# Slot sums copied and turned in halves, products in quarters with row products between, and one copy for the last outputs

## The chip, the cores and the metric

The kernel runs on one core of a Trainium2 chip. The metric is the device time of one execution in microseconds (us); of several runs the median is given. Five engines with an instruction queue each run beside one another: PE (matrix products; PEld is its weight load), DVE (vector), ACT (scalar functions and copies), POOL (a second elementwise engine) and SP, which here issues most loads and stores. Each engine takes its instructions strictly in the order in which the program gives them, and waits where one of them needs a result of another engine or of a transfer.

## The reference

Three layers stand one behind the other, all in float32:

```python
# 1 attention over 4 x 8 heads, 1152 keys, queries pooled by 2 (576), head size 64
attn_out = softmax(scale * mean_of_2(q) @ k.T) @ v          # -> x: 2304 tokens x 512
# 2 soft mixture of experts: 8 experts of 4 slots (32 slots), inner size 1024
logits = x @ phi
slot_input = softmax_over_tokens(logits).T @ x              # 32 x 512
slot_out[e] = relu(slot_input[e] @ w1[e]) @ w2[e]           # 32 x 512
x = softmax_over_slots(logits) @ slot_out                   # 2304 x 512
# 3 a gated layer, inner size 2048
h = x @ w_in
out = (h * cos(h)) @ w_out                                  # 2304 x 512
```

## The kernel before

The kernel doesn't form `x` of layer 3. Since `x @ w_in = softmax_over_slots(logits) @ (slot_out @ w_in)`, it computes the 32 x 2048 products `slot_out @ w_in` once (divided by 2 pi, tiles `Pst0` to `Pst3` of 512 columns each, with a rounded part and the rest stacked along the partitions) and multiplies them by the token weights `cT`.

Layers 1 and 2 are recorded by `attention()`; the order of their operations is written out in the string `ORDER`. At the end of layer 2 stand three operations that the change touches: `so_copy` copies the slot sums (32 slots, spread over four groups of partitions, 512 columns) from PSUM to SBUF (`so`), `so_turn` turns them by four products with a selection matrix (`gsel`), and `so_put` copies the result to SBUF as `soT`, four blocks of 128 x 128, one for each 128 of the 512 rows of `w_in` (index `kk`).

Layer 3 follows the table `START` for its beginning, and then a loop. The letters of the table:

- `p` (`p_some`): products of `soT` with the first 256 columns of `w_in` (`win_q`), in two column blocks of 128, in full width of the partitions. Each block is copied to `Pst0` by ACT, and its rest is formed by DVE.
- `r` (`p_rows`): the products of a whole half of `w_in`'s columns as four row groups of 32 partitions, ending in `p_hi` (ACT) and `p_lo` (DVE).
- `q` (`p_put`): spreads these by two products for each 256 columns (`s_hi`, `s_lo`) and copies them to a `Pst`.
- `s` (`split_w`): splits one of 16 blocks of `w_out` into a rounded part `w_hi` and the rest `w_lo`, on engines that `SPLIT` names: for blocks 0, 1, 2 `w_hi` is ACT's, `w_lo` is DVE's for 0 and POOL's for 1 and 2, and for block 3 `w_hi` is DVE's and `w_lo` POOL's.
- `u` (`emit_u`): product of `cT` and `Pst` for a unit of 128 or 256 inner columns and 256 tokens; ACT makes `t` from it, DVE `r`.
- `g` (`emit_g`): sine and square of `r` on ACT, `g` and its rounded part `hi` on DVE, the rest `lo` on POOL.
- `o` (`emit_o`): three products for each 128 inner columns and 128 tokens (`hi` with `w_hi`, `hi` with `w_lo`, `lo` with `w_hi`), summed over all units of a block of 256 tokens; at its end `store` copies the sums and sends them out.

All loads of layer 3 are issued by SP in the order of the program. The lines with their numbers:

Of the kernel before, what the change touches and what calls it, by code (L numbers as in the profile page):

```python
# [8 lines left out]
FP32 = mybir.dt.float32  # L9
# [22 lines left out]


START = (
# [106 lines left out]
def kernel(  # L141
# [77 lines left out]
    def mx():  # L219
        return mx2()[:, 0]  # L220

    def mx2():
        return ps_2.tile([128, 2, 512], FP32, tag=f"s{cur[0].spot}", name="mx")
# [804 lines left out]

    def so_copy(i):
        sh["so"] = ep.tile([128, DM], FP32, tag=f"E{cur[0].spot}", name="so")  # L1030
        nc.scalar.activation(out=sh["so"], in_=sh["o"], func=AF.Copy)

    def so_turn(i):
        sh["s"] = mx()
        for kk in range(HP):
            nc.tensor.matmul(
                out=sh["s"][:, kk * 128:(kk + 1) * 128], lhsT=sh["so"][:, kk * 128:(kk + 1) * 128],
                rhs=gsel.rearrange("p g s -> p (g s)"), start=True, stop=True,
            )

    def so_put(i):
        sh["soT"] = ep.tile([128, HP, 128], FP32, tag=f"E{cur[0].spot}", name="soT")
        nc.vector.tensor_copy(out=sh["soT"].rearrange("p k s -> p (k s)"), in_=sh["s"])

    def c_zero(b):
        sh["c", b] = mx()
# [449 lines left out]
    with tc.manual_schedule():  # L1496
# [51 lines left out]
        def load_win_q(f):  # L1548
            t = wo.tile([128, HP, 512], FP32, tag=f"w_lo{2 + f}", name="win_q")
            nc.sync.dma_start(out=t, in_=w32q[f])  # L1550
            for kk in range(HP):
                win_q[f, kk] = t[:, kk]
# [18 lines left out]

        for f in range(2):
            load_win_q(f)
            load_w(f, 2 - f)
        for i in range(HP // 2):
            nc.sync.dma_start(out=win1[:, i], in_=w32p[i].rearrange("p a b c -> p a (b c)"))

        ph = {}

        def p_some(f, c0, c1, pm):  # L1580
            pm = pm[:, 0:c1 - c0]
            for kk in range(HP):
                nc.tensor.matmul(
                    out=pm, lhsT=soT[:, kk, :],
                    rhs=win_q[f, kk][:, c0:c1], start=(kk == 0), stop=(kk == HP - 1),
                )
            nc.scalar.activation(out=Pst[f][:, c0:c1], in_=pm, func=AF.Copy, scale=INV2PI)
            lo = Pst[f][64:128, c0:c1]
            nc.vector.scalar_tensor_tensor(
                out=lo, in0=pm[64:128], scalar=INV2PI, in1=lo.bitcast(FP32), op0=ALU.mult, op1=ALU.subtract  # L1590
            )

        def p_rows(r, pm):
            pm = pm[:, 0:256]
            for kk in range(HP):
                for g in range(4):
                    c0 = g % 2 * 256
                    x = win1[:, kk // 2, kk % 2, g // 2 * 512 + c0:g // 2 * 512 + c0 + 256] if r else win_q[g // 2, kk][:, c0:c0 + 256]
                    nc.tensor.matmul(
                        out=pm[32 * g:32 * g + 32], lhsT=soT[:, kk, 0:32], rhs=x, start=(kk == 0), stop=(kk == HP - 1),  # L1600
                    )
            hi, lo = [op.tile([128, 256], F32R, bufs=1, tag=n, name=n) for n in ("p_hi", "p_lo")]
            nc.scalar.activation(out=hi, in_=pm, func=AF.Copy, scale=INV2PI)
            nc.vector.scalar_tensor_tensor(
                out=lo, in0=pm, scalar=INV2PI, in1=hi.bitcast(FP32), op0=ALU.mult, op1=ALU.subtract
            )
            ph[r] = hi, lo
# [58 lines left out]
        def emit_o(i):  # L1666
            blk, f0, n = units[i]
            hi, lo = gs.pop(i)
            last = i == len(units) - 1

            def product(s, f, part):
                ff = f0 + f
                if ff == 0 and part == 0:
                    acc[blk, s] = ps_o.tile([128, DM], FP32, tag=f"o{s}", name=f"o{s}")
                o = acc[blk, s]
                x = (lo if part else hi)[:, f, s * 128:(s + 1) * 128]
                nc.tensor.matmul(out=o, lhsT=x, rhs=w_hi[ff], start=(ff == 0 and not part), stop=bool(part and ff == NF - 1))  # L1677
                if not part:
                    nc.tensor.matmul(out=o, lhsT=x, rhs=w_lo[ff], start=False, stop=False)  # L1679

            def store(s):
                o = acc.pop((blk, s))
                ob = op.tile([128, DM], FP32, tag="ob", name="ob")
                if last:
                    h = DM // 2
                    nc.scalar.activation(out=ob[:, 0:h], in_=o[:, 0:h], func=AF.Copy, scale=-TWOPI)
                    nc.vector.tensor_scalar(out=ob[:, h:], in0=o[:, h:], scalar1=-TWOPI, scalar2=None, op0=ALU.mult)
                else:
                    nc.scalar.activation(out=ob, in_=o, func=AF.Copy, scale=-TWOPI)

                if blk < 2 * B:
                    runs = [(blk // 2, blk % 2 * TB + s * 128, 128)]
                else:
                    runs = [(2 * s + c, 512, 64) for c in range(2)]
                r0 = 0
                for b, c0, n in runs:
                    while n:
                        j, p0 = divmod(c0, QP)
                        w = min(n, QP - p0)
                        (nc.scalar if last and s and r0 else nc.sync).dma_start(  # L1700
                            out=out[b * SQ:(b + 1) * SQ, :].rearrange("(p j) d -> j p d", j=QJ)[j][p0:p0 + w],
                            in_=ob[r0:r0 + w],
                        )
                        r0, c0, n = r0 + w, c0 + w, n - w

            todo = [(s, f, part) for part in range(2) for f in range(n) for s in range(2)]
            for x in sorted(todo, key=lambda x: x[0]) if last else todo:
                product(*x)
                if last and x[1:] == (n - 1, 1):
                    store(x[0])  # L1710
            if f0 + n == NF and not last:
                for s in range(2):
                    store(s)

        def bank(i):
            return ps_o.tile([128, DM], FP32, tag=f"o{i}", name="pm")

        def emit_p(*a):
            p_some(*a, bank(1))

        def emit_r(r):
            p_rows(r, bank(0))
            if r == 0:
                for i in range(2, 4):
                    load_w(i)

# [49 lines left out]
```

## Time and profile before

| what | value |
|---|---|
| median of 3 runs | 733.82 us (733.76 to 736.04) |
| the profiled execution's own time | 736.87 us |
| its span, first to last instruction | 735.1 us |
| PE busy | 719.3 us (98%) |
| DVE, ACT, POOL busy | 573.0, 449.3, 418.5 us |

A profile is one execution with every instruction's start and duration. The span is a little shorter than the time of the same execution, and both may differ from the median of the runs, so a difference that is worked out from the profile is added to the median. A PE that is busy for 98% of the span is no proof that PE is at its peak everywhere: its instructions overlap, and what counts for an edit are the few places where PE waits.

### The profile page before, as it was taken

Reading aid. Unit: us, or ns where it says so; the run is one execution under the profiler, and the core shown is the slowest. Engines: PE = TensorE matmul, PEld = TensorE weight load, DVE = VectorE, ACT = ScalarE, POOL = GpSimd, SP = SyncE. Lnnn points to the kernel's source line nnn. Section 1 sums busy time; section 2 is a strip of 40 time slices with the busy share of each in tenths; the row PEclk is TensorE's granted clock in tenths of the full one; section 3 lists DMA queues with packets and bytes.
Section 4 is the critical chain, followed back from the end, with each engine's and each line's share of the span. In section 5 each row is a group of like instructions: output and inputs, shape, how many; then the busy total and the mean of one; then the engine's idle time right before and its main releaser. Section 6 shows DMA issues by size and latency. Waiting matters only on the chain.

```text
span 735.1 us, 16465 instructions
## 1 busy us (share of the span) xinstructions
PE 719.3 (98%) x6428; PEld 531.0 (72%) x6428; DVE 573.0 (78%) x917; ACT 449.3 (61%) x846; POOL 418.5 (57%) x351
## 2 busy tenths in 40 slices
PE   8999999999999999999999999998999999999997
PEld 7677767767677776777777676434778888888886
DVE  6999999989999999999999977404876665656562
ACT  5566666576566676567576555325676566666661
POOL 5676686775877746695767551314854444444442
PEclk9999999999999999999999999999999999999999
DMA  8455665575548646554633555999010010100101
GB/s 203 102 153 137 167 174 144 156 186 155 157 131 247 163 127 175 165 158 134 182 107 83 197 192 196 400 409 418 37 29 29 0 30 29 29 4 26 30 29 29
DMA packets 75970, 101.48 MB, mean 138 GB/s; under 512 B 47156, under 2 KB 47540, under 8 KB 74996
## 3 DMA queue, kind: packets, MB, share of 16 engines
q1 hardware_dynamic: 69872, 100.09, 44.9%
q10 hardware_dynamic: 6020, 0.34, 0.6%
q8 instruction: 51, 0.84, 0.5%
q14 instruction: 27, 0.22, 0.1%
HBM read 87.10 MB, written 13.11 MB: 136 GB/s over the span
## 4 chain that ended last, share of the span: by engine, by line
PE 82%; DVE 7%; DMA 4%; ACT 3%; issue 2%; POOL 2%; SPq 0%; ACTq 0%; POOLq 0%; DVEq 0%
PE mx L576 18%; PE o L1677 16%; PE mx L533 14%; PE o L1679 8%; PE mx L487 6%; PE mx L536 4%; PE u L1641 2%; DVE nm L496 2%; PE mx L990 2%; PE mx L514 2%; PE mx L447 1%; PE mx L606 1%; DMA w<-in_moe_w_dram 1%; PE mx L422 1%; PE mx L1023 1%
## 5 line engine op out<-in xcount | busy, mean ns | idle before, releaser
L565 POOL TENSOR_TENSOR ES<-ES,E 128x576 f32<-128x576 f32 (+2 forms) x154 | 224.5, 1459 | 66.3 <-DVE ES L565 39.3
L496 DVE TENSOR_REDUCE nm<-mx 128x2 f32<-128x768 f32 x240 | 221.4, 950 | 18.2 <-PE mx L487 16.9
L547 ACT ACTIVATE E<-mx 128x576 f32<-128x576 f32 (+2 forms) x288 | 174.8, 652 | 66.1 <-PE mx L536 46.1
L533 PE MATMUL mx<-Q,kX 64*128 64x288 f32 (+2 forms) x1152 | 164.3, 302 | 1.1 <-DVE nm L496 0.7
L576 PE MATMUL mx<-E,vn 128*64 128x288 f32 (+2 forms) x1152 | 158.0, 413 | 0.7 <-ACT part L818 0.4
L1661 POOL TENSOR_TENSOR lo<-g,hi 128x512 fp32r<-128x512 f32 (+1 forms) x73 | 94.0, 1287 | 109.3 <-DVE hi L1659 103.1
L533 PEld LDWEIGHTS mx<-Q,kX 64*128 64x128 f32 x1152 | 110.2, 184 | 13.7 <-issue 3.5
L576 PEld LDWEIGHTS mx<-E,vn 128*64 128x64 f32 x1152 | 75.3, 136 | 57.9 <-ACT E L547 5.8
L1677 PE MATMUL o<-w_hi,hi 128*128 128x512 f32 x288 | 113.0, 392 | 0.6 <-DVE hi L1659 0.6
L1679 PE MATMUL o<-w_lo,hi 128*128 128x512 f32 x288 | 113.1, 393 | 0.3 <-DVE w_lo L1568 0.3
L533 PE MATMUL mx<-Q,kY 64*128 64x288 f32 (+2 forms) x576 | 88.0, 292 | 0.0
L536 PE MATMUL mx<-NM,one_row 64*128 64x288 f32 (+2 forms) x576 | 87.8, 291 | 0.0
L487 PE MATMUL mx<-kX,Q 64*128 64x384 f32 x490 | 83.0, 368 | 0.9 <-ACT kX L460 0.6
L1646 ACT ACTIVATE t<-u 128x512 f32<-128x512 f32 (+1 forms) x73 | 42.9, 591 | 58.5 <-PE u L1641 58.4
L1657 DVE SCALAR_TENSOR_TENSOR g<-r,u 128x512 f32<-128x512 f32 (+1 forms) x73 | 49.6, 679 | 36.0 <-ACT r L1655 34.7
L1677 PE MATMUL o<-w_hi,lo 128*128 128x512 f32 x288 | 77.3, 389 | 0.0
L1648 DVE SCALAR_TENSOR_TENSOR r<-t,u 128x512 f32<-128x512 f32 (+1 forms) x73 | 49.3, 678 | 35.4 <-ACT t L1646 34.9
L319 POOL TENSOR_TENSOR cvt<-cvt 128x512 uint32<-128x512 uint32 x32 | 43.2, 1349 | 54.1 <-ACT E L547 19.4
L1677 PEld LDWEIGHTS o<-w_hi,lo 128*128 128x128 f32 x288 | 54.1, 188 | 11.3
L1677 PEld LDWEIGHTS o<-w_hi,hi 128*128 128x128 f32 x288 | 54.1, 188 | 10.8 <-DVE hi L1659 0.8
L1679 PEld LDWEIGHTS o<-w_lo,hi 128*128 128x128 f32 x288 | 54.2, 188 | 10.2 <-DVE w_lo L1568 0.6
L487 PEld LDWEIGHTS mx<-kX,Q 64*128 64x128 f32 x490 | 43.3, 184 | 23.0 <-issue 9.2
(231 smaller groups left out, 1023.5 us busy)
## 6 DMA issues: line engine op xcount, KB each, us to landing
w<-in_moe_w_dram SPq DMA_DIRECT2D x42, 512.0 KB
vn<-in_v_dram SPq DMA_DIRECT2D x16, 576.0 KB
qn<-in_q_dram SPq DMA_DIRECT2D x15, 576.0 KB
kn<-in_k_dram SPq DMA_DIRECT2D x15, 576.0 KB
raw<-in_moe_w_in_dram SPq DMA_DIRECT2D x16, 512.0 KB
raw<-in_moe_w_out_dram SPq DMA_DIRECT2D x16, 512.0 KB
hw<-in_moe_w_dram SPq DMA_DIRECT2D x23, 256.0 KB
lw<-in_moe_w_dram SPq DMA_DIRECT2D x10, 512.0 KB
```

The lines of the kernel that those rows point to most:

```text
L487: nc.tensor.matmul(out=m[:, h, 0:384], lhsT=Q1[p % 2][hs, AT[i]:AT[i] + 128], rhs=X[p][hs, ks], start=True, stop=True)
L496: nc.vector.tensor_reduce(out=nm3[p][:, i, :, c:c + 1], in_=m[:, :, 0:384], axis=AX.X, op=ALU.max)
L533: nc.tensor.matmul(out=sc[:, h, 0:n_q], lhsT=x[hs, ks], rhs=y[hs, qs], start=(n == 0), stop=False)
L536: nc.tensor.matmul(out=sc[:, h, 0:n_q], lhsT=one_row[hs, :], rhs=NM[p % 2][hs, qs], start=False, stop=True)
L547: nc.scalar.activation(out=e, in_=sc[:, :, 0:n_q], func=AF.Exp, scale=1.0 / 16.0)
L565: eng.tensor_tensor(out=ES[p, a], in0=ES[p, a], in1=E[p, a, t], op=ALU.add)
L576: nc.tensor.matmul(out=av_t[p, a, g][64 * h:64 * h + 64, 0:n_q], lhsT=vn[p][:, h, t, :], rhs=E[p, a, t][:, h, :], start=(t == g), stop=(t ...
L1648: nc.vector.scalar_tensor_tensor(out=r, in0=t, scalar=MAGIC, in1=u, op0=ALU.subtract, op1=ALU.subtract)
L1657: nc.vector.scalar_tensor_tensor(out=g, in0=r, scalar=1.0, in1=u, op0=ALU.subtract, op1=ALU.mult)
L1661: nc.gpsimd.tensor_tensor(out=lo[:, 0:n], in0=g, in1=hi[:, 0:n].bitcast(FP32), op=ALU.subtract)
L1677: nc.tensor.matmul(out=o, lhsT=x, rhs=w_hi[ff], start=(ff == 0 and not part), stop=bool(part and ff == NF - 1))
L1679: nc.tensor.matmul(out=o, lhsT=x, rhs=w_lo[ff], start=False, stop=False)
```

## The change

`so_copy` makes two copies of 256 columns on ACT. `so_turn` writes the four turned blocks to two banks of PSUM. `so_put` makes two copies of 256 columns, the first on ACT, the second on DVE. The first 256 columns' products (`p_first`) run over the first two `kk` for both column blocks and then over the last two. The row products of `r` 0 are split over `START`: one `kk` ahead of the first `u`, one ahead of the second, and two behind it; the entries `s` 1, `s` 2 and `s` 0 come later than the two `u`. Both halves of `win_q` are loaded first, the `w_out` blocks behind them. `store` copies the last outputs in one piece on ACT, as all others.

```diff
 START = (
-    ("s", 1), ("p", 0, 0, 128), ("s", 2), ("p", 0, 128, 256), ("u", 0), ("s", 0), ("u", 1), ("g", 0),
-    ("r", 0), ("s", 3), ("g", 1), ("q", 0, 1), ("q", 1, 2), ("u", 2), ("o", 0), ("s", 5), ("s", 6), ("s", 4), ("u", 3),
+    ("p",), ("r", 0, 0, 1), ("u", 0), ("s", 1), ("r", 0, 1, 2), ("u", 1), ("s", 2), ("s", 0), ("g", 0),
+    ("r", 0, 2, 4), ("s", 3), ("g", 1), ("q", 0, 1), ("q", 1, 2), ("u", 2), ("o", 0), ("s", 5), ("s", 6), ("s", 4), ("u", 3),
...
     def so_copy(i):
         sh["so"] = ep.tile([128, DM], FP32, tag=f"E{cur[0].spot}", name="so")
-        nc.scalar.activation(out=sh["so"], in_=sh["o"], func=AF.Copy)
+        for j in range(2):
+            cs = slice(j * DM // 2, (j + 1) * DM // 2)
+            nc.scalar.activation(out=sh["so"][:, cs], in_=sh["o"][:, cs], func=AF.Copy)
 
     def so_turn(i):
-        sh["s"] = mx()
+        sh["s"] = mx2()
...
-                out=sh["s"][:, kk * 128:(kk + 1) * 128], lhsT=sh["so"][:, kk * 128:(kk + 1) * 128],
+                out=sh["s"][:, kk // 2, kk % 2 * 128:(kk % 2 + 1) * 128], lhsT=sh["so"][:, kk * 128:(kk + 1) * 128],
...
-        nc.vector.tensor_copy(out=sh["soT"].rearrange("p k s -> p (k s)"), in_=sh["s"])
+        for j in range(2):
+            o, x = sh["soT"][:, 2 * j:2 * j + 2].rearrange("p k s -> p (k s)"), sh["s"][:, j, 0:256]
+            if j:
+                nc.vector.tensor_copy(out=o, in_=x)
+            else:
+                nc.scalar.activation(out=o, in_=x, func=AF.Copy)
...
         for f in range(2):
             load_win_q(f)
+        for f in range(2):
             load_w(f, 2 - f)
...
+        def p_first(pms):
+            for k0 in (0, 2):
+                for c, pm in enumerate(pms):
+                    cs = slice(128 * c, 128 * c + 128)
+                    for kk in range(k0, k0 + 2):
+                        nc.tensor.matmul(
+                            out=pm[:, 0:128], lhsT=soT[:, kk, :], rhs=win_q[0, kk][:, cs], start=(kk == 0), stop=(kk == HP - 1),
+                        )
+            for c, pm in enumerate(pms):
+                cs = slice(128 * c, 128 * c + 128)
+                nc.scalar.activation(out=Pst[0][:, cs], in_=pm[:, 0:128], func=AF.Copy, scale=INV2PI)
...
-        def p_rows(r, pm):
+        def p_rows(r, pm, k0=0, k1=HP):
             pm = pm[:, 0:256]
-            for kk in range(HP):
+            for kk in range(k0, k1):
...
+            if k1 < HP:
+                return
...
-                if last:
-                    h = DM // 2
-                    nc.scalar.activation(out=ob[:, 0:h], in_=o[:, 0:h], func=AF.Copy, scale=-TWOPI)
-                    nc.vector.tensor_scalar(out=ob[:, h:], in0=o[:, h:], scalar1=-TWOPI, scalar2=None, op0=ALU.mult)
-                else:
-                    nc.scalar.activation(out=ob, in_=o, func=AF.Copy, scale=-TWOPI)
+                nc.scalar.activation(out=ob, in_=o, func=AF.Copy, scale=-TWOPI)
```

The order of ACT's instructions from the slot sums' copy to `p_hi`, before (`w_hi1` is block 1's rounded part; `pm`, `mx` and `u` lie in PSUM):

```order
L1031 ACTIVATE so_7807<-mx_7710 128x512
L1566 ACTIVATE w_hi1_7851<-w_lo_7868 128x512
L1587 ACTIVATE Pst0_7835<-pm_7885 128x128
L1566 ACTIVATE w_hi2_7852<-w_lo_7868 128x512
L1587 ACTIVATE Pst0_7835<-pm_7894 128x128
L1646 ACTIVATE t_7903<-u_7901 128x256
L1566 ACTIVATE w_hi0_7850<-w_lo_7868 128x512
L1646 ACTIVATE t_7911<-u_7909 128x256
L1654 ACTIVATE r_7905<-r_7905 128x256
L1655 ACTIVATE r_7905<-r_7905 128x256
L1603 ACTIVATE p_hi_7940<-pm_7923 128x256
```

and after:

```order
L1033 ACTIVATE so_7807<-mx_7710 128x256 x2
L1050 ACTIVATE soT_7815<-mx_7810 128x256
L1598 ACTIVATE Pst0_7837<-pm_7885 128x128
L1598 ACTIVATE Pst0_7837<-pm_7886 128x128
L1659 ACTIVATE t_7906<-u_7904 128x256
L1573 ACTIVATE w_hi1_7853<-w_lo_7872 128x512
L1659 ACTIVATE t_7918<-u_7916 128x256
L1573 ACTIVATE w_hi2_7854<-w_lo_7872 128x512
L1573 ACTIVATE w_hi0_7852<-w_lo_7872 128x512
L1667 ACTIVATE r_7908<-r_7908 128x256
L1668 ACTIVATE r_7908<-r_7908 128x256
L1616 ACTIVATE p_hi_7942<-pm_7899 128x256
```

Half of `soT` has come to ACT, and `w_hi1` and `w_hi2` have moved from ahead of the two `Pst` copies to behind the first and the second `t`.

DVE's instructions in the same stretch after the change, with what each waits for (the engine's or the transfer's counter); before, the order was the same but for the first, which was one copy of 512 columns, and for the two in the middle, `w_lo` and the second `r`, which stood the other way round:

```order
L1048 COPY soT_7815<-mx_7810 128x256 [waits Activation_49]
L1600 SCALAR_TENSOR_TENSOR Pst0_7837<-pm_7885,Pst0_7837 64x128 [waits DMAHW4_49,Activation_49]
L1600 SCALAR_TENSOR_TENSOR Pst0_7837<-pm_7886,Pst0_7837 64x128 [waits Activation_49]
L1661 SCALAR_TENSOR_TENSOR r_7908<-t_7906,u_7904 128x256 [waits DMAHW2_49,Activation_49]
L1661 SCALAR_TENSOR_TENSOR r_7920<-t_7918,u_7916 128x256 [waits DMAHW3_49,Activation_49]
L1575 TENSOR_TENSOR w_lo_7872<-w_lo_7872,w_hi0_7852 128x512 [waits DMAHW2_49,DMAHW1_49,Activation_49]
L1670 SCALAR_TENSOR_TENSOR g_7928<-r_7908,u_7904 128x256 [waits Activation_49]
L1672 CAST hi_7930<-g_7928 128x256 [waits DMAHW7_49,DMAHW0_49,DVE_49]
L1617 SCALAR_TENSOR_TENSOR p_lo_7943<-pm_7899,p_hi_7942 128x256 [waits DMAHW6_49,Activation_49]
L1571 CAST w_hi3_7855<-w_lo_7872 128x512 [waits DMAHW3_49]
```

DVE's half of `soT` waits for ACT alone; `g` and `hi` stand ahead of `p_lo`, and `w_hi3` behind it, as before.

PE's instructions from the turn to the last row product, after (before, the 8 products of `p` stood in two blocks of 4, both `u` behind them, and the 16 of `r` behind both `u`):

```order
L1038 MATMUL mx_7810<-gsel_63,so_7807 128x128 x4
L1593 MATMUL pm_7885<-win_q_7868,soT_7815 128x128 x2
L1593 MATMUL pm_7886<-win_q_7868,soT_7815 128x128 x2
L1593 MATMUL pm_7885<-win_q_7868,soT_7815 128x128 x2
L1593 MATMUL pm_7886<-win_q_7868,soT_7815 128x128 x2
L1610 MATMUL pm_7899<-win_q_7868,soT_7815 32x256 x2
L1610 MATMUL pm_7899<-win_q_7870,soT_7815 32x256 x2
L1654 MATMUL u_7904<-cT0_7561,Pst0_7837 128x256
L1610 MATMUL pm_7899<-win_q_7868,soT_7815 32x256 x2
L1610 MATMUL pm_7899<-win_q_7870,soT_7815 32x256 x2
L1654 MATMUL u_7916<-cT0_7561,Pst0_7837 128x256
```

The first `u` now has all 8 products of `p` and 4 of the row products ahead of it. In the trace each of these float32 products is two pieces.

## Rows read from the trace of the kernel before

**Rows 1.** Head of the profile's page.
```profile
span 735.1 us, 16465 instructions
```

**Rows 2.** Chain of waits, 498 to 511 us: start, duration, what.
```profile
489.35 8.88 DMA w<-in_moe_w_dram
...
500.34 0.61 ACT so L1031
...
500.99 1.17 PE mx L1036 x8
...
503.00 2.07 PE pm L1583 x16
...
506.13 1.93 PE pm L1599 x32
```

**Rows 3.** Timeline of ACT: start, duration, instruction, [idle before, releaser].
```profile
502.03 0.63 ACT L1566 ACTIVATE w_hi<-w_lo 128x512 fp32r<-128x512 f32 x1 [1.09 <-DMA w_lo<-w32o]
504.20 0.28 ACT L1587 ACTIVATE Pst<-pm 128x128 fp32r<-128x128 f32 x1 [1.54 <-PE pm L1583]
...
505.27 0.38 ACT L1646 ACTIVATE t<-u 128x256 f32<-128x256 f32 x1
505.56 0.62 ACT L1566 ACTIVATE w_hi<-w_lo 128x512 fp32r<-128x512 f32 x1
...
506.45 0.41 ACT L1654 ACTIVATE r<-r 128x256 f32<-128x256 f32 x1
506.89 0.42 ACT L1655 ACTIVATE r<-r 128x256 f32<-128x256 f32 x1
508.09 0.38 ACT L1603 ACTIVATE p_hi<-pm 128x256 fp32r<-128x256 f32 x1 [0.78 <-PE pm L1599]
...
510.88 1.66 ACT L1566 ACTIVATE w_hi<-w_lo 128x512 fp32r<-128x512 f32 x3
```

**Rows 4.** Timeline of DVE, 500 to 532 us.
```profile
506.21 0.69 DVE L1568 TENSOR_TENSOR w_lo<-w_lo,w_hi 128x512 fp32r<-128x512 f32 x1
...
507.34 0.42 DVE L1657 SCALAR_TENSOR_TENSOR g<-r,u 128x256 f32<-128x256 f32 x1
507.80 0.29 DVE L1659 CAST hi<-g 128x256 fp32r<-128x256 f32 x1
508.51 0.42 DVE L1604 SCALAR_TENSOR_TENSOR p_lo<-pm,p_hi 128x256 fp32r<-128x256 f32 x1 [0.41 <-ACT p_hi L1603]
508.85 0.42 DVE L1564 CAST w_hi<-w_lo 128x512 fp32r<-128x512 f32 x1
...
509.71 1.06 DVE L1659 CAST hi<-g 128x256 fp32r<-128x256 f32 x1
...
514.97 0.72 DVE L1659 CAST hi<-g 128x512 fp32r<-128x512 f32 x1
...
526.10 1.66 DVE L1568 TENSOR_TENSOR w_lo<-w_lo,w_hi 128x512 fp32r<-128x512 f32 x1
```

**Rows 5.** Timeline of POOL, 500 to 532 us.
```profile
503.08 1.26 POOL L1568 TENSOR_TENSOR w_lo<-w_lo,w_hi 128x512 fp32r<-128x512 f32 x1 [10.05 <-ACT w_hi L1566]
...
508.23 0.73 POOL L1661 TENSOR_TENSOR lo<-g,hi 128x256 fp32r<-128x256 f32 x1 [1.88 <-PE pm L1599]
509.35 1.28 POOL L1568 TENSOR_TENSOR w_lo<-w_lo,w_hi 128x512 fp32r<-128x512 f32 x1 [0.39 <-DVE w_hi L1564]
...
511.60 3.80 POOL L1568 TENSOR_TENSOR w_lo<-w_lo,w_hi 128x512 fp32r<-128x512 f32 x3
...
527.17 1.74 POOL L1568 TENSOR_TENSOR w_lo<-w_lo,w_hi 128x512 fp32r<-128x512 f32 x1
```

**Rows 6.** Waits of PE, 516 to 735 us: total, times, longest.
```profile
PE u L1641 <- ACT Pst L1620: 0.7, 1, 0.7
```

**Rows 7.** Chain of waits, 720 us to the end.
```profile
730.50 0.39 ACT ob L1686
...
730.92 0.42 DVE ob L1687
```

More of the change, by code (lines that the diff above doesn't have):

```diff
@@ L1578 @@
         ph = {}
-        def p_some(f, c0, c1, pm):
-            pm = pm[:, 0:c1 - c0]
-            for kk in range(HP):
-                nc.tensor.matmul(
-                    out=pm, lhsT=soT[:, kk, :],
-                    rhs=win_q[f, kk][:, c0:c1], start=(kk == 0), stop=(kk == HP - 1),
-                )
[L1587 to L1591, printed above, removed]
-        def p_rows(r, pm):
+        def p_first(pms):
[9 more added lines that the diff above has]
+                nc.scalar.activation(out=Pst[0][:, cs], in_=pm[:, 0:128], func=AF.Copy, scale=INV2PI)
+                lo = Pst[0][64:128, cs]
+                nc.vector.scalar_tensor_tensor(
+                    out=lo, in0=pm[64:128, 0:128], scalar=INV2PI, in1=lo.bitcast(FP32), op0=ALU.mult, op1=ALU.subtract
+                )
+        def p_rows(r, pm, k0=0, k1=HP):
             pm = pm[:, 0:256]
-            for kk in range(HP):
+            for kk in range(k0, k1):
                 for g in range(4):
@@ L1716, in bank, with emit_p, emit_r @@
             return ps_o.tile([128, DM], FP32, tag=f"o{i}", name="pm")
[L1718 to L1723, printed above, removed]
+        def emit_p():
+            p_first([bank(1), bank(1)])
+        rows = {}
+        def emit_r(r, k0=0, k1=HP):
+            if k0 == 0:
+                rows[r] = bank(0)
+            p_rows(r, rows[r], k0, k1)
+            if r == 0 and k1 == HP:
                 for i in range(2, 4):
```

## Prediction

> **What bounds the kernel now.** The page's head gives a span of 735.1 us [rows 1]. The profiled execution took 736.87 us, so 1.8 us lie around its span; the median of the runs is 733.82, 3.05 below it. I work out a difference from the trace and add it to the median. Next I read the chain of waits around 500 us [rows 2], where PE stands still several times: the last weights of the slot sums land at 498.23, the sums are copied (`so`), turned by PE, copied again (`soT`), and the first factor's products follow, 16 pieces for two column blocks and then 32 for row group 0, which end at 508.06, just ahead of `p_hi`. Here PE waits for copies and copies wait for PE. Then I read ACT, DVE and POOL over the same stretch [rows 3 to 5], since between the copies these three convert the second factor's weights (`w_hi`, `w_lo`). Last, the waits of PE after 516 us: the longest is 0.7 [rows 6]. PE runs in order and has no slack behind that point, so whatever shifts PE at 516 arrives at the end, where a copy in two halves and a store follow [rows 7].
>
> **Halved copies and turns.** Before, from the start of `so` to the first product it is 500.34 to 503.00, 2.66 us [rows 2]. After: half of `so` on ACT, priced as `p_hi`, which is also 256 wide and read from PSUM, 0.38 [rows 3]; 0.05 to PE; the turn 1.17, since the second half of `so` ends 0.3 behind the first (ACT starts the next piece 0.29 after a 256-wide one, 505.27 to 505.56 [rows 3]) and is there in time; 0.08 to ACT; half of `soT` 0.38; 0.05 to PE. Sum 2.11, first product at 502.45: 0.55 won. The two halves of `soT` do not run side by side: in the order's rows DVE's half waits for ACT's alone, so it is ACT's that waits for all of the turn. That costs nothing here: DVE's half, priced as `p_lo` at 0.42 [rows 4], ends near 502.9, and the 8 products that need only ACT's half last to 503.4.
>
> **Quarters.** The first column block used to be complete after 8 of the 16 pieces, 1.20 us behind the first (503.00 to the `Pst` copy at 504.20 [rows 2, 3]). Now it takes 12. With 16 pieces in 2.07, four more are about 0.47, and the copy starts at 502.45 + 1.20 + 0.47 = 504.12. Of 0.55 won, 0.47 is spent.
>
> **Row products in between.** Before, that `Pst` copy and the first `t` copy on ACT lie 1.07 apart (504.20, 505.27 [rows 3]). After, that would give 505.19, but 8 of the 32 pieces stand on PE ahead of the product that `t` copies; at 1.93/32 = 0.06 each [rows 2] they last until about 504.9. I take 505.27 for `t` again, with 0.1 either way. All 32 pieces are then done near 507.0, a microsecond ahead of 508.06. This is what the edit could bring.
>
> **The conversions, moved in ACT's order.** Two of the three `w_hi` copies used to run before that `t`, one of them at 502.03 in time that ACT had to spare; now all three stand behind it. ACT starts the next piece 0.52 after a 512-wide copy (three in 1.66, the last of them 0.62 long [rows 3]). From `t` at 505.27: 0.29, `w_hi`1 at 505.56; 0.52, `t` of the second unit 506.08; 0.29, `w_hi`2 506.37; 0.52, `w_hi`0 506.89; 0.52, sine 507.41; 0.44, square 507.85; 0.29, `p_hi` at 508.14. Before it stood at 508.09 after 0.78 of waiting for PE. So ACT becomes what `p_hi` waits for, and the microsecond is gone.
>
> **The load order.** The second half of the first factor's columns is now loaded ahead of the second factor's first MB. From 498.23 to the end of ACT's wait at 502.03 [rows 2, 3] 1.5 MB landed, 2.53 us per MB. The two halves of `w_lo` then land at 504.55 and 505.8, and are wanted at 505.56 and 506.37: no cost, with 1.0 and 0.55 to spare.
>
> **DVE and POOL behind it.** `p_lo` on DVE followed `p_hi` at once, at 508.51, with `g` and `hi` done before it [rows 4]. Now the square ends at 508.27, and `g` (0.46 to the next) and `hi` (0.29) stand ahead of `p_lo`: by DVE's order alone it starts near 509.0, +0.5. On top of that, a DVE instruction from SBUF to SBUF that meets one of POOL's ends behind it: `hi` at 509.71 took 1.06 instead of 0.29 and ended 0.14 after POOL's 509.35 + 1.28; the 512-wide one at 514.97 ended 0.29 after POOL's three from 511.60 to 515.40; `w_lo` took 1.66 at 526.10 instead of the 0.69 at 506.21, and the POOL instruction begun at 527.17 ended 1.15 after it, having taken 1.74 [rows 4, 5].
>
> [...]
>
> POOL's `w_lo`1 follows the end of `w_hi`1 at 506.18 by 0.14 to 0.42 (as `lo` at 508.23 follows `hi`, and 503.08 follows the `w_hi` of 502.03), so it ends at 507.6 to 507.9, with `w_lo`2 right behind it. DVE wants to start `w_lo`0 at 507.55, nearly a tie. If DVE comes first, it ends at 508.2 to 508.5, `w_lo`2 1.15 later, and `hi` is held until then: `p_lo` 509.4 to 509.6. If POOL comes first, `w_lo`2 ends at 508.9, `w_lo`0 at about 509.5, and `p_lo` stands near 510.1. That is +0.9 to +1.55. A second meeting follows: `w_hi`3 came at 508.85 when `lo` was nearly done; now it comes some 0.1 after `lo` (0.73) has started, and waits for its end and 0.29 more: another 0.45. Then both engines run 1.35 to 2.0 late; so are POOL's three conversions and the `hi` of 514.97 that waits for them, and PE's next output products wait for that `hi`. PE has no other work in front of them that could cover this. I take **+1.6**, a little under the middle, since DVE's case is the nearer one.
>
> **The last store.** The last copy was 0.39 on ACT and then 0.42 on DVE, 730.50 to 731.34 [rows 7]. As one 512-wide copy it takes what `so` took, 0.61 [rows 2]: **-0.24**. The copy before it is covered by the output products that follow.
>
> **Sum.** +1.6 - 0.24 = about +1.35: a span of 736.4, and 733.82 + 1.35 = **735.2** for the median. A measurement of this kernel tells no change from one below about 0.3%, 2.2 us; by that I forecast no change.
>
> **Rivals.** (1) *DVE and POOL hardly meet*: only DVE's order remains, +0.5 - 0.24, **734.1**. For it: the tie hangs on a few tenths. Against: `hi` would have to find POOL idle while POOL has its conversions bunched. (2) *The microsecond arrives*: `p_hi` follows the row products at 507.1 and `p_lo` follows `p_hi`, -1.0 - 0.24, **732.6**. For it: PE is what `p_hi` waits for now. Against: ACT's order is fixed, so it needs `t` a microsecond earlier than worked out. (3) *Slower by more than a measurement misses*: the late halves of `w_lo` hold ACT. Landing after 506.37, the second half delays all of ACT behind it; from 507.25 on the sum passes +2.2 and the time 736.0. I put the case at **736.5**. For it: a whole MB is put in front of them. Against: the steady 2.53 us per MB.
>
> **Chances.** Forecast 0.55, rival (1) 0.2, (2) 0.12, (3) 0.13. Only (3) passes 0.3%; (2) stops at 0.17%. So slower 0.13, faster 0.03 for a gain that I don't see, and no change 0.84. The range, 732.5 to 736.3, reaches down to (2) and leaves out most of (3).
>
> **What would show it.** Right: `p_hi` still near 508.1 without a wait for PE before it; `p_lo` at 509.4 or later; a `hi` or `w_lo` on DVE of 1 us or more between 507 and 510; PE waiting more than a microsecond for `hi` at its second output products; a last copy of 0.6. Wrong: `p_hi` near 507; ACT waiting for a load of `w_lo`; or a `hi` of 0.29 between idle stretches of POOL.

## The result and the profile after

The changed kernel took 738.46 us (median of 6 runs, 736.28 to 740.23) against 734.52 for the kernel before (median of 6 runs, 733.76 to 736.04): a ratio of 1.0053, 95% interval 1.0031 to 1.0075. It is slower by half a per cent, outside the predicted range.

The profiled execution of the changed kernel is the fastest of its six, 736.28 us.

```profile
span 734.5 us, 16462 instructions
```

The instructions ahead of the slot sums' copy are the same in all kernels here, yet `so` starts anywhere between 497.4 and 500.3 us in their profiles (500.34 in [rows 2]). So I count from the start of `so`, 497.92 after. The timeline of ACT after the change answers to [rows 3]:

```profile
497.92 0.66 ACT L1033 ACTIVATE so<-mx 128x256 f32<-128x256 f32 x2 [8.17 <-PE mx L1023]
499.61 0.38 ACT L1050 ACTIVATE soT<-mx 128x256 f32<-128x256 f32 x1 [1.03 <-PE mx L1038]
501.69 0.28 ACT L1598 ACTIVATE Pst<-pm 128x128 fp32r<-128x128 f32 x1 [1.69 <-PE pm L1593]
...
503.02 0.38 ACT L1659 ACTIVATE t<-u 128x256 f32<-128x256 f32 x1 [0.61 <-PE u L1654]
503.30 0.62 ACT L1573 ACTIVATE w_hi<-w_lo 128x512 fp32r<-128x512 f32 x1
503.90 0.38 ACT L1659 ACTIVATE t<-u 128x256 f32<-128x256 f32 x1
504.19 1.14 ACT L1573 ACTIVATE w_hi<-w_lo 128x512 fp32r<-128x512 f32 x2
505.23 0.41 ACT L1667 ACTIVATE r<-r 128x256 f32<-128x256 f32 x1
505.66 0.42 ACT L1668 ACTIVATE r<-r 128x256 f32<-128x256 f32 x1
505.99 0.37 ACT L1616 ACTIVATE p_hi<-pm 128x256 fp32r<-128x256 f32 x1
```

From `t` on ACT runs without a pause, and `p_hi` stands at the end of that run, with no wait of its own in front: it comes 8.07 after `so`, where it came at 7.75. DVE and POOL in the same execution, answering to [rows 4, 5]:

```profile
505.36 1.76 DVE L1575 TENSOR_TENSOR w_lo<-w_lo,w_hi 128x512 fp32r<-128x512 f32 x1 [0.62 <-ACT w_hi L1573]
507.04 0.41 DVE L1670 SCALAR_TENSOR_TENSOR g<-r,u 128x256 f32<-128x256 f32 x1
507.48 0.29 DVE L1672 CAST hi<-g 128x256 fp32r<-128x256 f32 x1
507.69 0.42 DVE L1617 SCALAR_TENSOR_TENSOR p_lo<-pm,p_hi 128x256 fp32r<-128x256 f32 x1
508.02 0.90 DVE L1571 CAST w_hi<-w_lo 128x512 fp32r<-128x512 f32 x1
...
514.18 1.17 DVE L1672 CAST hi<-g 128x512 fp32r<-128x512 f32 x1
```

```profile
504.06 2.51 POOL L1575 TENSOR_TENSOR w_lo<-w_lo,w_hi 128x512 fp32r<-128x512 f32 x2 [13.41 <-ACT w_hi L1573]
507.91 0.73 POOL L1674 TENSOR_TENSOR lo<-g,hi 128x256 fp32r<-128x256 f32 x1 [1.34 <-issue]
```

POOL's two conversions take 2.51 together, so the second starts near 505.3. DVE's `w_lo` starts some 0.05 behind it and ends 0.55 after POOL: 1.76 us for what took 0.69. `p_lo` comes 9.77 after `so`, not 8.17. Then `w_hi` meets `lo` and takes 0.90 for 0.42. The timeline of PE shows what this does:

```profile
506.50 0.36 PE L1627 MATMUL pm<-p_hi,spread 128*128 128x256 f32 x1 [1.63 <-ACT p_hi L1616]
508.16 0.38 PE L1628 MATMUL pm<-p_lo,spread 128*128 128x256 f32 x1 [1.31 <-DVE p_lo L1617]
...
515.40 0.50 PE L1690 MATMUL o<-w_hi,hi 128*128 128x512 f32 x1 [0.32 <-DVE hi L1672]
...
527.50 0.50 PE L1692 MATMUL o<-w_lo,hi 128*128 128x512 f32 x1 [0.29 <-DVE w_lo L1575]
```

PE has finished the row products early and then stands for 1.63 and 1.31 us with one product in between. The output products that stood at 515.74 in the kernel before, 15.40 after `so`, come 17.48 after it. From here on I call them the third unit's output products. The row before:

```profile
515.74 0.50 PE L1677 MATMUL o<-w_hi,hi 128*128 128x512 f32 x1 [0.29 <-DVE hi L1659]
```

PE's last products, first of the kernel before and then of the changed one:

```profile
729.85 0.61 PE L1677 MATMUL o<-w_hi,lo 128*128 128x512 f32 x2
```

```profile
729.52 0.61 PE L1690 MATMUL o<-w_hi,lo 128*128 128x512 f32 x2
```

The last copy in the chain of waits at the end, answering to [rows 7]:

```profile
730.17 0.60 ACT ob L1697
```

| us after the start of `so` | before | after |
|---|---|---|
| first product | 2.66 | 2.13 |
| `t` of the first unit | 4.93 | 5.10 |
| `p_hi` / `p_lo` | 7.75 / 8.17 | 8.07 / 9.77 |
| third unit's output products | 15.40 | 17.48 |
| end of PE | 230.13 | 232.22 |
| end of PE to end of span | 4.62 | 4.36 |

The last two lines of the table give +2.09 - 0.26 = +1.83 for this execution. The medians differ by 3.94. So there are two questions: why 1.83 and not 1.35, and where some 2 us more come from that this profile doesn't show.

### The profile page after: what moved, and what is told of

Same layout as the page of the kernel before. It is cut to its first block, busy times and chain, and to the rows that moved or that the text cites. A ratio compares the mean times of both kernels' runs of the same rounds, so it can differ in the third digit from the quotient of the medians.

```text
span 734.5 us, 16462 instructions
## 1 busy us (share of the span) xinstructions
PE 719.2 (98%) x6428; PEld 530.4 (72%) x6428; DVE 573.4 (78%) x915; ACT 450.0 (61%) x848; POOL 418.6 (57%) x351
## 4 chain that ended last, share of the span: by engine, by line
PE 85%; DVE 6%; ACT 3%; issue 2%; DMA 2%; POOL 1%; SPq 0%; ACTq 0%; DVEq 0%; POOLq 0%
PE mx L576 19%; PE o L1690 16%; PE mx L533 15%; PE o L1692 8%; PE mx L487 6%; PE mx L536 5%; DVE nm L496 2%; PE u L1654 2%; PE mx L990 2%; PE mx L514 2%; PE mx L447 1%; PE mx L606 1%; DMA w<-in_moe_w_dram 1%; PE mx L422 1%; PE mx L1023 1%
```

## The experiments

Ratios are to runs of the kernel before on the same chip, with 95% intervals. Positions such as "at 7.91" or "+20.5" count from the start of `so`; the tail is the time from the end of PE to the end of the span. Three chips were used: one for the first four runs, one for the next four, one for the last four.

**1. The changed kernel again** (no edit).

> The changed kernel again, unedited. Theory A: of the 3.9 us that the change costs in the median, about 2.1 are lost where PE waits for hi at its second output products, 0.2 are won at the last copy, and the remaining 2 are a lower granted TensorE clock behind the new idle time of PE (1.6 and 1.3 us, shortly after one another): the mean clock is below 0.998 in most runs, and a profile with such a clock shows the fall within some microseconds of that place. Theory B: the remaining 2 us come from the attention part, which in two profiles of identical code differed by 2.4 us: then the clock is as high as in the kernel before and the median falls anywhere between 735 and 738.

Measured: 737.96, ratio 1.0038 (1.0024 to 1.0051). Its profiled execution took 738.52, 2.24 more than the first profile. The clock by stretches (columns: stretch, its length, busy time and instructions of PE, weight loads, DVE, ACT, POOL, then the granted clock, the share of the DMA engines and GB/s):

```profile
506.60:508.70 2.10, 0.79 (x4) 0.76 (x4) 2.06 (x6) 0.43 (x2) 0.72 (x1) 0.53 1.01 421
508.70:512.10 3.40, 3.40 (x12) 2.89 (x11) 2.67 (x5) 2.40 (x5) 3.04 (x3) 0.50 1.01 422
512.10:513.50 1.40, 1.40 (x7) 1.24 (x6) 0.04 (x1) 0.67 (x2) 1.40 (x2) 0.50 0.86 357
513.50:520.00 6.50, 6.50 (x54) 4.47 (x52) 5.18 (x10) 4.25 (x8) 4.26 (x5) 1.00 0.06 23
```

The same stretch in the first profile:

```profile
508.70:512.10 3.40, 3.19 (x17) 2.36 (x16) 2.90 (x5) 2.81 (x6) 2.82 (x3) 1.00 1.02 424
```

PE had just stood for 1.62 us and stands again when the granted clock goes to 0.50, until 513.5. The third unit's output products come 18.89 after `so`, 1.41 later than in the first profile. And further on PE meets a wait that was 0.29 there. The rows are of PE, DVE and POOL of this execution:

```profile
529.68 0.50 PE L1692 MATMUL o<-w_lo,hi 128*128 128x512 f32 x1 [1.18 <-DVE w_lo L1575]
```

```profile
521.26 1.55 DVE L1575 TENSOR_TENSOR w_lo<-w_lo,w_hi 128x512 fp32r<-128x512 f32 x1 [1.38 <-ACT w_hi L1573]
...
527.98 1.64 DVE L1575 TENSOR_TENSOR w_lo<-w_lo,w_hi 128x512 fp32r<-128x512 f32 x1
```

```profile
520.97 1.29 POOL L1575 TENSOR_TENSOR w_lo<-w_lo,w_hi 128x512 fp32r<-128x512 f32 x1
```

And DVE and POOL at the same place in the first profile of the changed kernel:

```profile
520.09 0.69 DVE L1575 TENSOR_TENSOR w_lo<-w_lo,w_hi 128x512 fp32r<-128x512 f32 x1 [1.07 <-ACT w_hi L1573]
```

```profile
520.10 1.83 POOL L1575 TENSOR_TENSOR w_lo<-w_lo,w_hi 128x512 fp32r<-128x512 f32 x1
```

There DVE's `w_lo` (block 11) starts 0.01 ahead of POOL's (block 7) and takes 0.69; here DVE is 1.38 later after `so` and POOL 1.08, so POOL is 0.29 ahead, DVE takes 1.55, and DVE's later `w_lo` of block 8, for which PE waits, is late. The change didn't make this near tie: it stands in the kernel before too, where DVE is 0.02 ahead.

```profile
520.41 0.69 DVE L1568 TENSOR_TENSOR w_lo<-w_lo,w_hi 128x512 fp32r<-128x512 f32 x1 [1.07 <-ACT w_hi L1566]
```

```profile
520.43 1.83 POOL L1568 TENSOR_TENSOR w_lo<-w_lo,w_hi 128x512 fp32r<-128x512 f32 x1
```

1.41 + 0.89 = 2.30 of the 2.41 by which PE ends later here than in the first profile (234.63 after `so`, against 232.22).

**2. The kernel before again** (no edit).

> The kernel before, unedited, for the clock and span of each of its runs. Theory A: the mean clock is 0.998 in nearly all runs, as PE never idles for more than 0.9 us there, and the runs lie within 2 us. Theory B: clocks of 0.995 to 0.997 appear here as often as in the changed kernel.

Measured: 735.45, ratio 1.0004 (0.9993 to 1.0016). End of PE 230.14 after `so`, tail 4.61, the same as in the first profile to 0.02, with `so` starting at 497.39: the 2.95 us by which that first profile began later lie ahead of the change. One of these 12 runs has a clock of 0.997 and none a lower one, so theory B falls; theory A's spread of 2 us is too narrow, the runs reach from 733.74 to 737.35.

**3. The last store in one piece, alone** (the kernel before with the last hunk of the diff).

> The kernel before with one edit: the last outputs leave by one copy on ACT. Both theories: 0.24 us faster, 0.03%, too little to tell from none by time; in the profile the time from the end of PE to the end of the span is shorter by 0.24.

Measured: 734.85, ratio 0.9998 (0.9986 to 1.0010). The tail is 4.35: -0.26, lost in the spread of the runs. This execution shows that the kernel before can lose its clock too: 0.50 in the stretch from 501.0 to 504.4, and end of PE at 231.58 instead of 230.13.

**4. The changed kernel with PE's idle time filled.** 21 products into a spare buffer, which leave the output as it is.

```diff
+            d = ps_u.tile([128, UF, TB], FP32, tag="u", name="u") if n == 1 else None
+            def fill(k):
+                for _ in range(k):
+                    nc.tensor.matmul(
+                        out=d[:, 0], lhsT=Pst[0][:, 0:128], rhs=cT[0][:, 0:256], start=True, stop=True
+                    )
+            if n == 1:
+                fill(12)
...
                 nc.tensor.matmul(out=o, lhsT=s_hi[:, g, :], rhs=hi, start=True, stop=False)
+                if n == 1:
+                    fill(9)
                 nc.tensor.matmul(out=o, lhsT=s_lo[:, g, :], rhs=lo, start=False, stop=True)
```

> The changed kernel with 21 idle products on PE (12 ahead of the first spreading product, 9 between it and its second half), written to a PSUM buffer that nobody reads, so that PE works through its new idle time; outputs are unchanged. Theory A: the 2.1 us at the second output products stay, the clock stays at 0.998 or above, and the median falls to about 736 to 736.5. Theory B: clock and median are those of the changed kernel, 738.

PE's timeline with the fill:

```profile
505.17 1.69 PE L1629 MATMUL u<-cT,Pst 128*128 128x256 f32 x12
...
507.06 1.23 PE L1629 MATMUL u<-cT,Pst 128*128 128x256 f32 x9
508.57 0.39 PE L1641 MATMUL pm<-p_lo,spread 128*128 128x256 f32 x1 [0.28 <-DVE p_lo L1617]
```

Measured: the granted clock is 0.999 to 1.0 in all 12 runs, where 6 of the 9 runs of experiment 1 have 0.997 or less, so the idle time does cause the fall. But the median only goes to 737.62, not to theory A's 736 to 736.5; the ratio is 1.0031 (1.0019 to 1.0043), which can't be told from experiment 1's by time. Five runs took 735.9 to 736.7, seven 737.6 to 738.7. The profiled one (737.69) is of the seven and has the other loss. DVE's and POOL's `w_lo`:

```profile
520.49 1.84 DVE L1575 TENSOR_TENSOR w_lo<-w_lo,w_hi 128x512 fp32r<-128x512 f32 x1 [1.10 <-ACT w_hi L1573]
```

```profile
520.49 1.29 POOL L1575 TENSOR_TENSOR w_lo<-w_lo,w_hi 128x512 fp32r<-128x512 f32 x1
```

They start in the same hundredth, PE waits 1.18 at block 8 and ends 233.25 after `so`. What puts the two level here isn't shown; it may be the filling itself. Filling cures the clock, and by itself it brings no time that the runs can show.

**5. Filled, and the tie of the two `w_lo` moved.** Block 7's conversion goes behind block 11's.

```diff
-    ("g", 4), ("s", 7), ("o", 2), ("q", 2, 2), ("s", 11), ("u", 5),
+    ("g", 4), ("o", 2), ("q", 2, 2), ("s", 11), ("s", 7), ("u", 5),
```

> The changed kernel with the 21 PE products that fill its new idle time, and with block 7's conversion moved behind block 11's in START, so that DVE's w_lo (20.07 after the start of so before, 22.16 after) no longer starts within 0.02 us of a POOL w_lo (20.09 and 22.18). The filled kernel without this move ran at full clock in all its runs, yet at 735.9 to 738.7, median 737.62, and its profile shows POOL ahead at that place, DVE's w_lo 1.84 long instead of 0.69 and PE 0.9 later from 30 us on. Theory A (that tie is the rest of the loss): clocks stay at 0.999 to 1.0, the long times go, median 735.9 to 736.4, ratio about 1.002; end of PE 232.1 to 232.4 after the start of so. Theory B (what is left over full clock comes from elsewhere, the attention part or a later meeting): the times still spread up to 738.5 and the median stays near 737.6.

Measured: 736.92, ratio 1.0016 (1.0004 to 1.0028), clocks 0.998 to 1.0. The ratio came as theory A has it, the microseconds did not, since before took 735.92 on this chip. The tie is gone, but block 8's `w_lo` is still a little late: PE waits 0.69, and ends 232.62 after `so`, above the 232.1 to 232.4 expected.

**6. Only the conversions late** (the kernel before with two entries moved).

```diff
-    ("s", 1), ("p", 0, 0, 128), ("s", 2), ("p", 0, 128, 256), ("u", 0), ("s", 0), ("u", 1), ("g", 0),
+    ("p", 0, 0, 128), ("p", 0, 128, 256), ("u", 0), ("s", 1), ("u", 1), ("s", 2), ("s", 0), ("g", 0),
```

> The kernel before with nothing changed but START's entries s 1 and s 2, which come behind the first and the second u, as after the change. Theory A (the move of the conversions makes the loss at the first output products): ACT is what p_hi waits for, at +8.1 to 8.6 after the start of so instead of +7.75, p_lo at +9.8 to 10.3 instead of +8.17 with a DVE w_lo or hi of 1 us or more in front of it, the third unit's output products at +17.4 to 17.9 instead of +15.4, and the median 2.3 us or more above before, since PE's idle time is there as well: 736.8 to 739. Theory B (it is the products' new order or the halved copies that lose it): these stay within 0.3 of before, median 734.3 to 735.2.

DVE and POOL in this execution (`so` at 499.48):

```profile
506.77 0.83 DVE L1568 TENSOR_TENSOR w_lo<-w_lo,w_hi 128x512 fp32r<-128x512 f32 x1 [0.61 <-ACT w_hi L1566]
507.52 0.42 DVE L1657 SCALAR_TENSOR_TENSOR g<-r,u 128x256 f32<-128x256 f32 x1
507.98 0.90 DVE L1659 CAST hi<-g 128x256 fp32r<-128x256 f32 x1
508.79 0.41 DVE L1604 SCALAR_TENSOR_TENSOR p_lo<-pm,p_hi 128x256 fp32r<-128x256 f32 x1
```

```profile
505.75 2.98 POOL L1568 TENSOR_TENSOR w_lo<-w_lo,w_hi 128x512 fp32r<-128x512 f32 x2 [13.96 <-ACT t L1646]
```

Measured: 737.58, ratio 1.0019 (1.0005 to 1.0033). `p_hi` at 7.91, `p_lo` at 9.31, the third unit's products at 17.02: +1.62, less than the 2.0 to 2.5 expected, because DVE's `w_lo` gets in ahead of POOL's second conversion here: POOL's two take 2.98 instead of 2.51, and `hi` is held afterwards (0.90 instead of 0.29). PE ends at 231.74, +1.61. DVE first and POOL first were the prediction's two cases; the changed kernel has the other one. Theory B, which had this kernel at the time of before, falls: the moved conversions alone make a loss of this kind and most of its size.

**7. Conversions behind `p_hi`.** The changed kernel with block 0 right behind the first `t`, blocks 1 and 2 behind `p_hi`, and 3, 5, 6, 4 later still.

```diff
-    ("p",), ("r", 0, 0, 1), ("u", 0), ("s", 1), ("r", 0, 1, 2), ("u", 1), ("s", 2), ("s", 0), ("g", 0),
-    ("r", 0, 2, 4), ("s", 3), ("g", 1), ("q", 0, 1), ("q", 1, 2), ("u", 2), ("o", 0), ("s", 5), ("s", 6), ("s", 4), ("u", 3),
-    ("g", 2), ("u", 4), ("o", 1), ("g", 3), ("r", 1), ("g", 4), ("s", 7), ("o", 2), ("q", 2, 2), ("s", 11), ("u", 5),
+    ("p",), ("r", 0, 0, 1), ("u", 0), ("s", 0), ("r", 0, 1, 2), ("u", 1), ("g", 0),
+    ("r", 0, 2, 4), ("g", 1), ("q", 0, 1), ("s", 1), ("q", 1, 2), ("u", 2), ("s", 2), ("o", 0), ("s", 3), ("u", 3),
+    ("g", 2), ("u", 4), ("s", 5), ("o", 1), ("g", 3), ("r", 1), ("s", 6), ("s", 4), ("g", 4), ("s", 7), ("o", 2), ("q", 2, 2), ("s", 11), ("u", 5),
```

> The changed kernel with START in another order: block 0's conversion right behind the first t, those of blocks 1 and 2 behind p_hi, those of 3, 5, 6 and 4 behind the second and third units' steps. Theory A (products and copies in pieces do bring a microsecond, and the conversions take it back): p_hi at about +7.1 after the start of so, waiting for PE and not for ACT, p_lo at +7.5 to 7.9, no DVE instruction over 1 us ahead of p_lo, the third unit's output products at +14.5 to 15.0 instead of +15.4 before and +17.5 after, median 733.4 to 734.2, 0.4 to 1.2 below before. Theory B (the pieces bring nothing, or POOL's conversions hold hi wherever they stand): these products at +15.4 or later, and the median at before's or above.

PE's timeline (`so` at 498.47):

```profile
506.04 0.36 PE L1627 MATMUL pm<-p_hi,spread 128*128 128x256 f32 x1 [0.62 <-ACT p_hi L1616]
506.76 0.39 PE L1628 MATMUL pm<-p_lo,spread 128*128 128x256 f32 x1 [0.37 <-DVE p_lo L1617]
...
513.19 0.50 PE L1690 MATMUL o<-w_hi,hi 128*128 128x512 f32 x1
...
520.12 0.50 PE L1692 MATMUL o<-w_lo,hi 128*128 128x512 f32 x1 [1.16 <-POOL w_lo L1575]
```

Measured: 736.38, ratio 1.0010 (0.9996 to 1.0024). Up to the third unit all is as theory A has it: `p_hi` at 7.04, the output products at 14.72, 0.68 ahead of before. Then PE waits 1.16 for POOL's `w_lo` of block 4 and 1.05 for block 8's, and ends at 231.79. What the row products bring, 0.7 us, is there, and is lost to conversions that are now late; the median, 2.2 above the top of theory A's range, shows no gain.

**8. The halved copies and turns alone** (the kernel before with the hunks of `so_copy`, `so_turn`, `so_put`).

> The kernel before with nothing changed but the halved copies of so and soT and the turn in two banks. Both theories: first product at +2.13 after the start of so instead of +2.66. Theory A: that half microsecond reaches PE's first-unit products but is taken up at the row products, which then wait for the second half of win_q, or arrives as at most 0.5 at the end: median 734.0 to 734.6, ratio 0.999 to 1.000. Theory B (the halves upset the meeting of DVE and POOL by themselves): p_lo and the third unit's output products 1 us or more late, median 735.5 or more.

Measured: 734.90, ratio 0.9988 (0.9975 to 1.0001). First product at 2.13, `p_hi` at 7.44, end of PE at 229.83: 0.30 of the half microsecond arrives at the end. The interval includes 1, so the runs alone don't show the gain.

**9. The changed kernel on the third chip** (no edit), beside the next run.

> The changed kernel, unedited, on the same chip as the next one. Of its 15 runs so far two came at a granted clock of 1.0 (735.8 and 736.28), the others at 0.994 to 0.998 (736.95 to 740.23). Theory A (PE's new idle time of 1.6 and 1.3 us ahead of the first output products lets the clock fall, and a tie of DVE and POOL at 22 us is lost in some executions): again most runs at 0.998 or below and 2 to 3 us above before, median ratio 1.003 to 1.005. Theory B (the clocks of those two sets were the chip's or the hour's): clocks as those of before, 0.998 to 1.0, and a ratio near 1.0025, the +1.83 of the undisturbed profiles.

Measured: 737.81, ratio 1.0038 (1.0022 to 1.0055), three of six runs at a clock of 0.994 to 0.996. In the profiled one the clock is 0.50 from 508.7 to 512.1:

```profile
508.70:512.10 3.40, 3.40 (x10) 2.82 (x11) 2.46 (x4) 2.15 (x4) 3.12 (x4) 0.50 1.02 424
```

The third unit's products come at 18.20 (+0.72 against the first profile), POOL is again 0.29 ahead of DVE at the near tie, PE waits 1.18 at block 8 and ends at 233.91: 232.22 + 0.72 + 0.89 = 233.83.

**10. Filled, the tie moved in another way.** Block 11's conversion goes ahead of the third output products, so that DVE's `w_lo` queues behind POOL's `lo`.

```diff
-    ("g", 4), ("s", 7), ("o", 2), ("q", 2, 2), ("s", 11), ("u", 5),
+    ("g", 4), ("s", 7), ("s", 11), ("o", 2), ("q", 2, 2), ("u", 5),
```

> The changed kernel with the 21 filling products and with block 11's conversion moved ahead of the third output products, so that ACT makes its w_hi some 2 us earlier and DVE's w_lo queues behind a POOL lo instead of starting level with a POOL w_lo. Theory A (with full clock and without the tie only the +1.83 of the undisturbed profiles is left): clocks 0.999 to 1.0, ratio to before 1.0015 to 1.0025 and at least 0.0012 below that of the unedited changed kernel beside it; in the profile end of PE 231.9 to 232.3 after the start of so, and a wait for w_lo at 29 us of 0.3 or less. Theory B: no difference from the kernel beside it that the intervals can tell.

Measured: 736.84, ratio 1.0021 (1.0012 to 1.0030), clocks 0.998 to 1.0. The wait at block 8 is 0.30, PE ends at 232.30. That is what theory A expects of the profile and of the ratio, 0.0017 below the unedited kernel beside it, and the median is 1.85 above before's, where the undisturbed profile has +1.83. The two intervals still overlap (1.0022 to 1.0030), though in 58 of the 66 pairs of one run of each the unedited kernel is the slower; so the runs make this likely and the profiles show the mechanism.

**11. The conversions of experiment 7 in another order.** Block 4 ahead of 5 and 6; blocks 8 and 14 change places. Parts of two lines of `START`, against experiment 7:

```diff
-("s", 5), ("o", 1), ("g", 3), ("r", 1), ("s", 6), ("s", 4), ("g", 4)
+("s", 4), ("o", 1), ("g", 3), ("r", 1), ("s", 5), ("s", 6), ("g", 4)
...
-("q", 3, 2), ("s", 14), ("g", 5), ("o", 3), ("s", 8)
+("q", 3, 2), ("s", 8), ("g", 5), ("o", 3), ("s", 14)
```

> The version with p_hi at +7.04 and the third unit's output products at +14.72 (0.7 ahead of before) lost that again by two waits of PE for w_lo, 1.16 at +20.5 (block 4, which POOL converted last of 5, 6 and 4) and 1.05 at +28.1 (block 8). Here block 4 comes ahead of 5 and 6, and blocks 8 and 14 change places. Theory A (the won microsecond is only moved to the next conversion that comes late): no wait at +20.5, 0 to 1.0 at +26 to 28 for hi or w_lo, end of PE 229.6 to 230.8 after the start of so against 230.13 before, ratio 0.998 to 1.0005. Theory B (POOL's and DVE's conversions as a whole bound this stretch, so that any order ends alike): end of PE at 231.5 or later, ratio 1.001 or more.

PE and DVE:

```profile
523.26 0.50 PE L1692 MATMUL o<-w_lo,hi 128*128 128x512 f32 x1 [1.02 <-POOL w_lo L1575]
...
534.03 0.47 PE L1654 MATMUL u<-cT,Pst 128*128 128x256 f32 x2 [1.70 <-DVE g L1670]
```

```profile
528.22 2.95 DVE L1571 CAST w_hi<-w_lo 128x512 fp32r<-128x512 f32 x2
```

Measured: 737.05, ratio 1.0031 (1.0021 to 1.0040), end of PE 232.57. My theory fell here. The wait for block 4 is gone and others are there: 1.02 for another `w_lo` of POOL's, 1.70 for `g`, which stands behind two DVE casts of 2.95 together that meet POOL (one took 0.42 at 508.85 in [rows 4]). Of two orders both lost the gain within 20 us of the third unit. That no order keeps it isn't shown.

**12. Halved copies and the last store together.** The kernel before with the two edits of experiments 3 and 8.

> The kernel before with the halved copies and turns and the last store in one piece, without the products' order and the loads. The halves alone ended PE 229.83 after the start of so (230.13 before), the one copy alone left 4.35 to 4.36 behind PE (4.61 before). Theory A (both add up and nothing else moves): first product +2.13, p_hi +7.4, end of PE 229.8, tail 4.35, together 0.55 below before, ratio 0.9985 to 0.9998. Theory B: the gain is lost at the third unit's output products or by a lower clock, ratio 1.0 or more.

PE's timeline (`so` at 497.59):

```profile
499.72 2.06 PE L1590 MATMUL pm<-win_q,soT 128*128 128x128 f32 x16 [0.53 <-ACT soT L1050]
...
512.68 0.50 PE L1684 MATMUL o<-w_hi,hi 128*128 128x512 f32 x1 [0.29 <-DVE hi L1666]
```

Measured: 734.12 against 734.99, ratio 0.9985 (0.9976 to 0.9994). End of PE 229.84, tail 4.39: 0.5 less than before by the profile. This version is faster than both kernels, by about as much as can be told. The halved copies may help in another way: none of the 23 runs of experiments 8 and 12 has a clock of 0.997 or less, against 21 of 107 of the kernel before, and PE's wait ahead of the first product is 0.53 here instead of 0.85. That this wait is the reason isn't shown.

## Why the prediction was wrong

- *Halved copies*: right. Worked out 2.11 to the first product, measured 2.13; alone they leave 0.30 at the end (experiment 8).
- *Quarters, row products, conversions*: right in kind, and the gain came out smaller. The first `Pst` copy is 0.09 earlier (3.77 after `so` instead of 3.86; worked out 0.08). The row products are done 0.7 earlier (6.95 instead of 7.66; worked out 1.0), and nobody uses them: `t` came at 5.10 where I had 4.93, ACT's chain behind it was read to 0.1, and `p_hi` came at 8.07 where it gave 7.80. Experiment 7 shows that it is this chain which keeps `p_hi` back: without the two conversions in it `p_hi` comes at 7.04.
- *Load order*: right. ACT has no wait for a load among its conversions, and rival (3) did not come.
- *The last store*: right, -0.26 for -0.24.
- *DVE and POOL behind it*: the meeting came as worked out, its size did not. I took +1.6, "since DVE's case is the nearer one", out of 1.35 to 2.0. POOL came first, by some 0.05: `p_lo` +1.60, the second meeting +0.48, the output products **+2.08**, as my end of 2.0 for that case has it. I had worked out one end for each of two cases, and the middle is neither. Both cases have been seen: POOL first, +2.08, after the change; DVE first, +1.62 where I had 1.35, in experiment 6, a kernel without the halved copies. One sign I had named was off: PE waits for `p_hi` and `p_lo`, 1.63 and 1.31, and only 0.32 for `hi` at the third unit.
- *The step that failed*: the sum, +1.6 - 0.24, took "whatever shifts PE at 516 arrives at the end" for all that arrives. In the undisturbed profile it is all, +2.08 at 516 and +2.09 at the end. But the late PE is idle PE, and I priced its idle time by its length alone and put the clock at nothing. The new idle time lowers the clock: at 0.997 or below were 14 of the 21 runs of the changed kernel, none of the 35 runs with the idle time filled, and 21 of 107 of the kernel before. In the two profiles of the changed kernel that hold the fall it cost 1.41 and 0.72. And in both it cost 0.89 more further on, as the late PE and what ACT copies for it put DVE 0.29 behind POOL at the near tie 22 us after `so`: 1.18 of wait instead of 0.29. In the six profiles of other kernels with this part of `START` as it was and no fall behind `p_hi` DVE stays 0.01 to 0.03 ahead. It is lost at full clock in one profile, of the filled kernel; that it is ever lost at full clock in the changed kernel isn't shown.

Together: 1.83 + 0.72 + 0.89 = 3.4 to 1.83 + 1.41 + 0.89 = 4.1 where the clock falls, 1.83 where it doesn't; the medians lie 2.8 to 3.9 above those of before. The runs' own clocks agree: the three runs of the changed kernel at 1.0 took 735.8 to 736.5, the median of the 14 at 0.997 or below is 738.5. Of the 3.3 us between 735.2 and the measured 738.46, 0.5 is the size of the meeting of DVE and POOL, 0.7 the median to which I added (733.82 of three runs, 734.52 of six), and about 2.1 is what the profile of the fastest run doesn't show and the profiles of experiments 1 and 9 put down to the clock and what follows from it.

What stays open: how the runs at full clock with the idle time filled still reach 738.7, and one run of the changed kernel at 0.998 740.21. The start of `so`, which wanders by almost 3 us in these profiles, would be enough for much of it, but none of these runs has a profile.

## What to carry to other kernels

A product that is ready earlier is worth nothing while the copy that fetches it waits in another engine's order; and what is pushed back to make room there, here three conversions, is priced by the engines that meet behind it (DVE's `w_lo` took 1.76 us for 0.69). New idle time on TensorE had to be priced twice here, as the wait (1.63 and 1.31 us) and as the lower clock that may follow it (0.50 in two profiles, for 1.41 and 0.72 us more). A few filling products (21 here) tell whether the clock is part of the loss; here they didn't show its price, since the filled kernel had another loss further on. Where two engines can hold each other up, as DVE and POOL did here, look for starts within hundredths of each other all along the way behind an edit, not at the edit alone, and in the kernel before as well: a tie that every profile of it shows won may be lost once one of the two is late.

## What the runs showed of the hardware

- The granted clock fell to 0.50 at two waits of PE of about 1.6 and 1.3 us with one product between them, in some executions and not in others of the same program: during the second wait in experiment 1, about 1 us behind it in experiment 9, and not at all in the first profile. 512-wide products then started 0.43 apart instead of 0.23. With the idle time filled none of 35 runs has a clock below 0.998; of the 21 runs of the changed kernel 14 have 0.997 or less. What sets the moment of the fall, and how long it lasts (about 6.8 us in experiment 1, 3.4 in experiment 9), isn't shown.
- Which of DVE and POOL took longer turned on hundredths: started at 520.09 and 520.10, DVE took 0.69 and POOL 1.83; both at 520.49 to the hundredth, DVE took 1.84 and POOL 1.29. What makes the one longer beside the other isn't shown.
